# An adaLN block with linear attention: TensorE's order in phase 1 written out, state products in pairs, and x of the MLP's second pair loaded half a step sooner

## The chip, the cores and the metric

The kernel runs on one core of one Trainium2 chip. The metric is device time in microseconds; smaller is better. Before the change the median of three runs is 778.76 us (778.49 to 779.13). The engines are TensorE (PE, with its weight loads listed as PEld), VectorE (DVE), ScalarE (ACT), GpSimd (POOL) and SyncE (SP), which only issues DMAs here. Each engine works off its own list of instructions in order, and waits on semaphores for the others.

## The reference

The block gets 2048 tokens of width 640 and a conditioning vector c. All is float32.

```python
mod = (silu(c) @ w_mod).reshape(1, 6, 1, 640)
sa, ca, ga, sb, cb, gb = (mod[:, i] for i in range(6))
h = layernorm(x) * (1 + ca) + sa
x = x + ga * A(h)                  # attention
h = layernorm(x) * (1 + cb) + sb
x = x + gb * B(h)                  # MLP

def A(x):                          # 32 heads of 20
    q, k, v = heads(x @ wqkv)
    pq, pk = q @ w_phi, k @ w_phi
    phi_q = concat(softmax(pq), softmax(-pq))
    phi_k = concat(softmax(pk), softmax(-pk))
    kv = einsum("bhsf,bhsd->bhfd", phi_k, v)
    z = sum over tokens of phi_k
    o = (phi_q @ kv) / (phi_q . z + 1e-6)
    return o @ wo

def B(x):                          # F = 1728
    r = relu(x @ w1 + b1)
    return (r * r) @ w2 + b2
```

## The kernel before

The tokens stand in 16 tiles of 128 (`NT`), and two tiles make a pair `j`. Float32 products are made of three float32r products (`three`): both operands are split into a high part and a low remainder, and high x high, high x low and low x high are summed. So a projection of one token tile to 640 columns is 30 matmuls: two column parts of 384 and 256 (`CUT`), five chunks of the width, three products.

*Phase 1* folds `w_phi` into the weights of Q and K and then goes through the token tiles t. For each it makes K (`proj("k", t)`, copied by `to_sb`), V (`do_v`) and, for the first twelve, Q (`do_q`); the last four Q are postponed (`POSTPONED`). `spread` subtracts each head's maximum and minimum on VectorE, `exps` takes the exponentials on ScalarE, `k_norm` sums a key's 64 softmaxes and divides, `q_sums` sums a query's and takes the reciprocal into `rs_q`; the query's exponentials go to DRAM (`ESP`) undivided and are loaded again in phase 2 (`load_e`). `do_kv(t)` adds tile t's keys times values to the state, which stays in three PSUM banks (`kvp`, line 448): 11 products with 64 columns of weights, each two records in the profile. `t1(j, ...)` transposes the normalised x of a pair (tile `ta`), scales it on ScalarE and splits it into `hT`, the operand of the projections; all transposes go through one PSUM bank, `tp`. `ln_parts` is the layer norm of a pair.

Beside that, phase 1 makes four of the six modulation vectors (2, 3, 4 and 5; `mod_acc`, `mac`): five loads of 128 rows of `w_mod` each, accumulated on VectorE into one row tile with tag `s1`, of which there are five buffers, and then either summed over the partitions by a product with ones (`mod_rows`, tile `mr`, for the gates 2 and 5) or transposed and summed (`to_cols`, tile `mc`, for 3 and 4, the shift and scale of the second layer norm). It also scales `wo` with the gate and splits it (`prep_wo`). All this is one generator, `sides`, of which each token tile takes three steps (`SIDES`).

In the loop over t = 2 to 13 the order on every engine is the planner's: it goes by the order of the program, the buffers, and its own reckoning of when an operand is ready. `tc.issue_after(i)` keeps an instruction behind instruction i on its engine. From tile 14 on the order on TensorE, VectorE, ScalarE and GpSimd is written out by hand (`manual_schedule`), as it is ahead of the loop.

*Phase 2* takes the queries. `make_z` spreads the sums of the keys over the partitions (`zb`), `e_prod(t)` multiplies a query's exponentials by them and sums over each head (`dn`), GpSimd makes the denominator from it (`dd`), `e_recip` inverts it, `e_scale` scales the exponentials into `ezb`, and `tr_e` transposes them on TensorE (tile `te`) for the products with the state (`num`) and with `wo` (`do_wo`). The result of a tile goes to DRAM (`A1`).

*The MLP* takes the pairs j = 0 to 7. A pair has 14 half steps, each with one product up (`up`, 15 matmuls, then relu and square) and a part of one product down. For pairs 0 and 1 these are plain (`down_plain`). During pair j the next pair is made ready by `layer`: load the attention's result (`load_xm`) and x (`load_xx`), add them and store the sum (`add_x`, line 1019), normalise in six ScalarE passes (`ln_pieces`: two sums, two squares, two scalings), and transpose (`t2`, tile `tb`). A table gives the half step of each: `LN_AT0` is the one for the preparation of pair 1 during pair 0. `PREPS` says how many weight chunks are split and loaded in each half step of pair 0 (`prep`: split high, split low, load). SP's order is written out in pair 0 too.

Of the kernel before, what the change touches and what calls it, by code (L numbers as in the profile page):

```python
# [11 lines left out]
AF = mybir.ActivationFunctionType  # L12
# [3 lines left out]
P = 128  # L16
# [19 lines left out]
SIDES = 3  # L36
# [15 lines left out]
def kernel(  # L52
# [245 lines left out]
    def to_cols(acc, dest, nm):  # L298
        for c0, n in ((0, 4), (4, 1)):
            p = tp(f"mc{nm}_{c0}")  # L300
            for i in range(n):
                nc.tensor.transpose(p[:, i * P : (i + 1) * P], acc[:, (c0 + i) * P : (c0 + i + 1) * P], ident)
            nc.vector.tensor_reduce(
                dest[:, c0 : c0 + n], p[:, : n * P].rearrange("p (a b) -> p a b", b=P), axis=AX.X, op=ALU.add
            )
# [6 lines left out]
    def mod_acc(part):  # L312
        acc = None
        for k in range(NC):
            t = stage(part * D, k)
            mac(t, t, k, acc)
            acc = t
            yield None
        yield acc

    def mod_cols(part, dest):
        for acc in mod_acc(part):
            if acc is None:
                yield
        to_cols(acc, dest, part)
        yield

    def mod_rows(part, dest):
        for acc in mod_acc(part):
            if acc is None:  # L330
                yield
        for h in range(2):
            p = tp(f"mr{part}_{h}")
            nc.tensor.matmul(p[:, :HALF], ones, acc[:, h * HALF : (h + 1) * HALF], start=True, stop=True)
            nc.scalar.activation(dest[:, h * HALF : (h + 1) * HALF], p[:, :HALF], AF.Copy)
        yield
# [51 lines left out]
    def t1(j, *ds):  # L388
        if 0 in ds:
            HT[j] = ht(f"hT{j}", j)  # L390
        p = tp(f"ta{j}_{ds[0]}")
        for k, d in enumerate(ds):
            t_in(XB[j], d, p[:, 256 * k : 256 * k + 256])
        for k, d in enumerate(ds):
            t_out(cols_a, HT[j], d, f"a{j}", p[:, 256 * k : 256 * k + 256])

# [17 lines left out]
    def do_v(t):  # L414
        p = proj("v", t)
# [57 lines left out]
    def q_sums(t):  # L473
# [3 lines left out]
        nc.vector.reciprocal(s, s)  # L477
# [5 lines left out]
    def prep_wo(g, ga_b):  # L483
# [13 lines left out]
        nc.vector.tensor_tensor(t[:m], t[:m], ga_b[:m], op=ALU.mult)  # L497
# [5 lines left out]
    def side():  # L503
        ga_b = row("s4", "ga_b")
        yield from mod_rows(2, ga_b)
        for g in range(NG):
            prep_wo(g, ga_b)
            yield
        yield from mod_cols(3, cols_b[:, 0:5])
        yield from mod_cols(4, cols_b[:, 5:10])  # L510
        nc.vector.tensor_scalar(cols_b[:, 5:10], cols_b[:, 5:10], 1.0, None, op0=ALU.add)
        yield from mod_rows(5, gb_b)
        t = row("s1", "b2s")
        nc.sync.dma_start(t, bass.AP(tensor=b2.tensor, offset=b2.offset, ap=[[0, P], [1, D]]))
        nc.vector.tensor_tensor(bb, t, gb_b, op=ALU.mult)
        nc.sync.dma_start(b1_t, b1)
        yield

    sides = side()


# [154 lines left out]
    for e in (ET_.PE, ET_.DVE, ET_.Activation, ET_.Pool, ET_.SP):  # L676
        behind.enter_context(tc.issue_after(last[e]))
    q_chain(0)
    do_kv(0)
    k_norm(EK[1], 1)  # L680
    q_chain(1)
    for t in range(2, NT - 2):
# [4 lines left out]
        to_sb(proj("k", t), PK[t])  # L687
        norm = j + 1 if i == 0 and t < NT - 4 else j + 2 if t == NT - 5 else None
# [4 lines left out]
        do_v(t)  # L693
        if norm:
            next(parts)
        if t >= NT - 4:
            for ds in (((0, 1), (2, 3)) if i == 0 else ((4,),)):
                t1(j + 1, *ds)
# [16 lines left out]
        for _ in range(SIDES):  # L715
            next(sides, None)
    for _ in sides:
        pass
# [23 lines left out]
    exps(EQ[q0])  # L742
    q_sums(q0)
# [76 lines left out]
    def e_prod(t):  # L820
# [7 lines left out]
        nc.gpsimd.tensor_tensor(dn, dn, rs, op=ALU.mult)  # L828
        dd = DD[t] = small([P, H], "dd", f"dd{t}")
        nc.gpsimd.tensor_tensor(dd, dn[:, 0], dn[:, 1], op=ALU.add)  # L830
        nc.gpsimd.tensor_scalar(dd, dd, 1e-6, None, op0=ALU.add)

    def e_recip(t):
# [4 lines left out]
        nc.vector.tensor_tensor(DN[t], rs, DD[t][:, None, :].to_broadcast([P, 2, H]), op=ALU.mult)  # L838
# [568 lines left out]
    LN_AT0 = {"load": 3, "xx": 4, "add": (6, 7), "ln": (6, 7, 8, 8, 9, 9), 10: (0, 1), 11: (2, 3), 12: (4,)}  # L1407
# [3 lines left out]
    PREPS = iter([1, 3] + [2, 1] * 2 + [2, 2] + [1, 1] + [1, 2])  # L1411
# [198 lines left out]
```

## Time and profile before

| | us |
|---|---|
| median of three runs | 778.76 |
| lowest and highest | 778.49, 779.13 |
| profiled execution | 778.49 |
| its span, first to last instruction | 776.8 |
| TensorE busy | 768.9 |
| VectorE busy | 585.0 |
| ScalarE busy | 440.3 |
| GpSimd busy | 123.9 |

By stretches, phase 1's loop and its end stand between about 52 and 257 us, phase 2 from there to about 398 us, the MLP behind it. The page's rows give busy times; the timeline merges neighbouring instructions of one kind into a row with its start, its length and the count, and names in brackets the idle time ahead of it and what ended it. Matmuls are pipelined: the length of a row of matmuls reaches past the start of the next one, so the distance between two starts is what a row costs.

### The profile page before, as it was taken

How to read it: one execution, taken by the hardware profiler on the slowest of the kernel's cores; microseconds unless marked ns; L12 is line 12 of the kernel's file. 1: busy time of each engine (PE TensorE's matmuls, PEld its weight loads, DVE VectorE, ACT ScalarE, POOL GpSimd, SP SyncE). 2: the span in 40 equal slices, each digit the busy share in tenths (PEclk: the TensorE clock that was granted, in tenths of full speed). 3: DMA queues.
4: the chain of work that ended last, by engine and by line, in shares of the span. 5: the costliest groups of instructions: out<-in, count | busy, mean ns of one | idle time of the engine just before them, and what ended most of it. 6: DMA issues, size and time to landing. Idle time of an engine off the chain costs nothing.

```text
span 776.8 us, 15295 instructions
## 1 busy us (share of the span) xinstructions
PE 768.9 (99%) x5989; PEld 745.3 (96%) x5989; DVE 585.0 (75%) x1059; ACT 440.3 (57%) x991; POOL 123.9 (16%) x253
## 2 busy tenths in 40 slices
PE   9999999999999999999999999999999999999997
PEld 9999999999999988998999999999999999999997
DVE  6699899998788799986266667776767567585656
ACT  5766685486663355665875737446454645536331
POOL 3001101001100233221000001122221313213110
PEclk9999999999999999999999999999999999999999
DMA  9713245323120254222247456997666858667450
GB/s 331 294 68 132 84 143 169 133 99 108 69 101 3 88 168 170 85 85 103 85 135 256 137 174 226 290 318 251 187 195 205 236 178 261 188 191 209 128 172 35
DMA packets 50551, 126.03 MB, mean 162 GB/s; under 512 B 5991, under 2 KB 6759, under 8 KB 50479
## 3 DMA queue, kind: packets, MB, share of 16 engines
q1 hardware_dynamic: 33144, 83.99, 31.2%
q0 software_dynamic: 14752, 35.76, 16.5%
q10 hardware_dynamic: 2583, 5.30, 1.8%
q8 instruction: 47, 0.77, 0.4%
q14 instruction: 25, 0.20, 0.1%
HBM read 95.05 MB, written 29.88 MB: 161 GB/s over the span
## 4 chain that ended last, share of the span: by engine, by line
PE 96%; ACT 2%; DVE 1%; DMA 0%; issue 0%; SPq 0%; POOL 0%; ACTq 0%; POOLq 0%
PE up L78 23%; PE acc L78 17%; PE pwo L78 10%; PE pq L78 9%; PE pk L78 9%; PE pv L78 9%; PE acc3x L78 5%; PE kvp L448 3%; PE te L865 2%; PE tb L364 1%; PE numa L78 1%; PE foldk L280 1%; PE numc L78 1%; PE numb L78 1%; PE ta L364 1%; PE foldq L280 1%
## 5 line engine op out<-in xcount | busy, mean ns | idle before, releaser
L78 PE MATMUL up<-h,w 128*128 128x256 f32 x1640 | 206.5, 278 | 0.2 <-ACT ft L1184 0.2
L78 PEld LDWEIGHTS up<-h,w 128*128 128x128 f32 x1640 | 196.1, 188 | 0.3 <-ACT ft L1184 0.3
L1184 ACT ACTIVATE ft<-up,b_t 128x256 f32<-128x256 f32 x104 | 49.1, 472 | 116.0 <-PE up L78 115.5
L78 PE MATMUL acc<-w,ra 128*128 128x384 f32 x452 | 98.2, 336 | 0.0
L1185 DVE TENSOR_TENSOR ft<-ft 128x256 f32<-128x256 f32 x104 | 44.1, 424 | 54.2 <-ACT ft L1184 52.5
L78 PE MATMUL pwo<-wo,ot 128*128 128x256 f32 (+3 forms) x512 | 81.1, 312 | 0.0
L78 PE MATMUL pk<-wk,hT 128*128 128x384 f32 (+1 forms) x480 | 77.8, 312 | 0.2 <-ACT hT L376 0.2
L78 PEld LDWEIGHTS pwo<-wo,ot 128*128 128x128 f32 (+1 forms) x512 | 75.0, 188 | 2.7 <-issue 2.7
L78 PE MATMUL pv<-wv,hT 128*128 128x384 f32 (+1 forms) x480 | 75.9, 309 | 0.0
L78 PE MATMUL pq<-wq,hT 128*128 128x384 f32 (+1 forms) x480 | 74.9, 311 | 0.4 <-ACT k L424 0.4
L78 PEld LDWEIGHTS pk<-wk,hT 128*128 128x128 f32 x480 | 71.9, 188 | 1.9 <-ACT hT L376 0.8
L78 PEld LDWEIGHTS acc<-w,ra 128*128 128x128 f32 x452 | 72.6, 188 | 1.0 <-DVE ra L88 0.8
L78 PEld LDWEIGHTS pq<-wq,hT 128*128 128x128 f32 x480 | 70.8, 188 | 1.6 <-ACT k L424 0.9
L78 PEld LDWEIGHTS pv<-wv,hT 128*128 128x128 f32 x480 | 70.7, 188 | 0.4
L88 DVE TENSOR_TENSOR ra<-ft,ra 128x384 fp32r<-128x384 f32 (+2 forms) x86 | 36.8, 449 | 32.8 <-ACT ra L1208 20.2
L78 PE MATMUL acc3x<-w,ra 128*128 128x256 f32 x248 | 42.4, 278 | 0.0
L1208 ACT ACTIVATE ra<-ft 128x384 fp32r<-128x384 f32 x48 | 25.2, 526 | 28.4 <-DVE ft L1185 22.4
L78 PEld LDWEIGHTS acc3x<-w,ra 128*128 128x128 f32 x248 | 39.8, 188 | 0.2 <-DVE ra L88 0.2
L1294 POOL DMA_DIRECT2D ring_a<-td_a x34 | 18.2, 536 | 124.3 <-PE acc L78 102.7
L1199 DVE TENSOR_TENSOR ft<-ft 128x128 f32<-128x128 f32 x136 | 33.4, 287 | 1.2
L476 DVE TENSOR_REDUCE rs_q<-eq 128x64 f32<-128x1280 f32 x16 | 23.5, 1476 | 11.1 <-ACT eq L435 11.1
L828 POOL TENSOR_TENSOR dn<-dn,rs_q 128x64 f32<-128x64 f32 x16 | 8.7, 543 | 131.1 <-DVE dn L826 131.1
(256 smaller groups left out, 1414.2 us busy)
## 6 DMA issues: line engine op xcount, KB each, us to landing
ring_c<-td_c POOLq DMA_DIRECT2D x34, 384.0 KB, 4.1
ring_a<-td_a POOLq DMA_DIRECT2D x34, 384.0 KB, 4.0
ring_b<-td_b POOLq DMA_DIRECT2D x34, 256.0 KB, 3.8
esp<-eq SPq DMA_DIRECT2D x12, 640.0 KB, 2.9
el<-esp SPq DMA_DIRECT2D x12, 640.0 KB, 4.0
rw<-in_w SPq DMA_DIRECT2D x23, 320.0 KB, 3.3
wm<-in_w_mod SPq DMA_DIRECT2D x20, 320.0 KB, 3.9
xb<-in_x SPq DMA_DIRECT2D x8, 640.0 KB, 4.0
```

The costliest lines, as they stand in the source:

```text
L78: nc.tensor.matmul(o, a, b, start=first and i == 0, stop=last and i == len(terms) - 1, skip_group_check=skip,)
L88: (eng or nc.vector).tensor_tensor(out_lo, full, hi.bitcast(F32), op=ALU.subtract)
L280: nc.tensor.matmul(p[g // 3][:, (g % 3) * 120 : (g % 3) * 120 + n], r, bd_t[:120, g * 120 : g * 120 + n], start=True, stop=True,)
L364: nc.tensor.transpose(p[:, i * P : (i + 1) * P], xn[:, i, d * P : (d + 1) * P], ident)
L448: nc.tensor.matmul(kvp[g // 4][64 * c : 64 * c + 64, a : a + 2 * n].rearrange("p (s n) -> p s n", s=2), v[:, u], e[:, :, o : o + n], start ...
L476: nc.vector.tensor_reduce(s, heads(flat(e)), axis=AX.X, op=ALU.add)
L865: nc.tensor.transpose(p[:m, a : a + P], EU[2 * j + i][:, b : b + m], ident)
L1184: nc.scalar.activation(r, p, AF.Relu, bias=b1_t[:, f : f + 1])
L1185: nc.vector.tensor_tensor(r, r, r, op=ALU.mult)
L1199: nc.vector.tensor_tensor(t[:, o], t[:, a], t[:, b], op=op)
L1208: nc.scalar.activation(a[:, 0, :3], t[:, :3], AF.Copy)
L1294: nc.gpsimd.dma_start(RING[j, n, r], TD[n][r].bitcast(F32R))
```

## The change

1. **TensorE's order in the loop of phase 1 is written out** (`manual_schedule` for TensorE alone). For each tile: K, V, Q, with the transposes at stated places. The other engines' order stays with the planner.
2. **State products in pairs.** For even t, `do_kv(t - 2)` and `do_kv(t - 1)` follow the matmuls of V(t), and V's copies stand behind them. Tiles 12 and 13 are paired after K(15). Keys 14 and 15 use the query buffers `q0`, `q1`.
3. **Modulation at stated tiles.** The generator is gone. A table `SIDE` says which loads and accumulations a tile makes, now in the order 3, 4, gate 2, `wo`, gate 5. The accumulations and the products with the gate stay behind the newest VectorE instruction. The transposes of 3 and 4 follow the state products of t = 6 and 10 (four columns) and the transposes in Q(7) and Q(11) (the fifth); ScalarE copies them to a row tile, and one sum on VectorE replaces two. The gate's row products follow the state products of t = 8 and K(9); those of gate 5 stand behind K(15) and Q(12).
4. **No reciprocal of q's sums.** `rs_q` holds the sums. With sums r0, r1 and products n0, n1 the denominator becomes r0 r1 1e-6 + n0 r1 + n1 r0, six GpSimd operations instead of three, and each half is scaled by the other half's sum, two VectorE operations of 32 instead of one of 64.
5. **MLP.** During pair 0, x of pair 1 is loaded in half steps 2 and 3 instead of 3 and 4, added in 5 and 6 instead of 6 and 7, and normalised from 5 to 9 instead of 6 to 9; one weight preparation moves from half step 6 to 5.

```diff
+    def mod_turn(part, p, *cs_):
+        t = MT.setdefault(part, None) or row("s1", f"mt{part}")
+        MT[part] = t
+        a, n = cs_[0] * P, len(cs_) * P
+        for i, c in enumerate(cs_):
+            nc.tensor.transpose(p[:, i * P : (i + 1) * P], MA[part][:, c * P : (c + 1) * P], ident)
+        nc.scalar.activation(t[:, a : a + n], p[:, :n], AF.Copy)
+    def mod_sum(part, dest):
+        with tc.issue_after(newest(ET_.DVE)):
+            nc.vector.tensor_reduce(dest, MT[part].rearrange("p (a b) -> p a b", b=P), axis=AX.X, op=ALU.add)
+    def mod_mac(part, *ks):
+        for k, t in [(k, stage(part * D, k)) for k in ks]:
+            with tc.issue_after(newest(ET_.DVE)):
+                mac(t, t, k, MA.get(part))
+            MA[part] = t
+    def mod_row(part, dest, h):
+        p = tp(f"mr{part}_{h}")
+        c = slice(h * HALF, (h + 1) * HALF)
+        nc.tensor.matmul(p[:, :HALF], ones, MA[part][:, c], start=True, stop=True)
+        nc.scalar.activation(dest[:, c], p[:, :HALF], AF.Copy)
...
     def q_sums(t):
...
-        nc.vector.reciprocal(s, s)
...
+    AFTER_KV = {
+        6: lambda: mod_turn(3, tp("mc3"), 0, 1, 2, 3),
+        8: lambda: mod_row(2, ga_b, 0),
+        10: lambda: mod_turn(4, tp("mc4"), 0, 1, 2, 3),
+        12: lambda: t1(NT // 2 - 1, 2, 3),
+    }
+    LAST_COL = {7: (3, cols_b[:, 0:5]), 11: (4, cols_b[:, 5:10])}
+    SIDE = {
+        2: lambda: mod_mac(3, 0, 1, 2),
+        3: lambda: (mod_mac(3, 3, 4), mod_mac(4, 0)),
+        4: lambda: mod_mac(4, 1, 2),
+        5: lambda: (mod_mac(4, 3, 4), mod_mac(2, 0)),
+        6: lambda: mod_mac(2, 1, 2, 3),
+        7: lambda: mod_mac(2, 4),
+        8: lambda: None,
+        9: lambda: wo_weights(0, 1),
...
+        13: lambda: (mod_mac(5, 3, 4), biases()),
+    }
...
-    do_kv(0)
-    k_norm(EK[1], 1)
     q_chain(1)
+    pe = tc.manual_schedule(engines={ET_.PE})
+    pe.__enter__()
     for t in range(2, NT - 2):
...
         to_sb(proj("k", t), PK[t])
+        if t == NT - 4:
+            t1(j + 1, 0, 1)
+        if t == 9:
+            mod_row(2, ga_b, 1)
...
-        do_v(t)
+        p = proj("v", t, (1, 0, lambda: t1(j + 1, 4)) if t == NT - 3 else None)
+        if i == 0:
+            do_kv(t - 2)
+            do_kv(t - 1)
+            if t in AFTER_KV:
+                AFTER_KV[t]()
+        v_out(t, p)
...
         if i and t < NT - 4:
             t1(j + 1, 2, 3)
-            t1(j + 1, 4)
...
-        do_kv(t - 1)
         if t < NT - POSTPONED:
-            do_q(t)
+            do_q(t, (1, 3, lambda: t1(j + 1, 4, more=LAST_COL.get(t))) if i else None)
             q_chain(t)
         if i == 0 and t < NT - 4:
             t1(j + 1, 0, 1)
-        for _ in range(SIDES):
-            next(sides, None)
+        SIDE[t]()
+    pe.__exit__(None, None, None)
...
-        EK[t] = tok2("k", f"ek{t}")
+        EK[t] = tok2(f"q{t % 2}", f"ek{t}")
         spread(PK[t], EK[t], f"k{t}")
+    do_kv(ka - 2)
     do_kv(ka - 1)
+    mod_row(5, gb_b, 0)
     exps(EK[ka])
     k_norm(EK[ka], ka)
     do_q(q0)
+    mod_row(5, gb_b, 1)
...
     exps(EQ[q0])
+    nc.vector.tensor_tensor(bb, b2s[0], gb_b, op=ALU.mult)
     q_sums(q0)
...
-        nc.gpsimd.tensor_tensor(dn, dn, rs, op=ALU.mult)
         dd = DD[t] = small([P, H], "dd", f"dd{t}")
-        nc.gpsimd.tensor_tensor(dd, dn[:, 0], dn[:, 1], op=ALU.add)
-        nc.gpsimd.tensor_scalar(dd, dd, 1e-6, None, op0=ALU.add)
+        nc.gpsimd.tensor_tensor(dd, rs[:, 0], rs[:, 1], op=ALU.mult)
+        nc.gpsimd.tensor_scalar(dd, dd, 1e-6, None, op0=ALU.mult)
+        for s in range(2):
+            nc.gpsimd.tensor_tensor(dn[:, s], dn[:, s], rs[:, 1 - s], op=ALU.mult)
+            nc.gpsimd.tensor_tensor(dd, dd, dn[:, s], op=ALU.add)
...
         nc.vector.reciprocal(DD[t], DD[t])
-        nc.vector.tensor_tensor(DN[t], rs, DD[t][:, None, :].to_broadcast([P, 2, H]), op=ALU.mult)
+        for s in range(2):
+            nc.vector.tensor_tensor(DN[t][:, s], rs[:, 1 - s], DD[t], op=ALU.mult)
...
-    LN_AT0 = {"load": 3, "xx": 4, "add": (6, 7), "ln": (6, 7, 8, 8, 9, 9), 10: (0, 1), 11: (2, 3), 12: (4,)}
+    LN_AT0 = {"load": 2, "xx": 3, "add": (5, 6), "ln": (5, 6, 7, 7, 8, 9), 10: (0, 1), 11: (2, 3), 12: (4,)}
...
-    PREPS = iter([1, 3] + [2, 1] * 2 + [2, 2] + [1, 1] + [1, 2])
+    PREPS = iter([1, 3] + [2, 1, 2, 2, 1, 2] + [1, 1] + [1, 2])
```

More of the change, by code (lines that the diff above doesn't have):

```diff
@@ L296, in mac @@
             nc.vector.scalar_tensor_tensor(acc, t, cs[:, k : k + 1], prev, op0=ALU.mult, op1=ALU.add)
[L298 to L305, printed above, removed]
+    MT = {}
+    def mod_turn(part, p, *cs_):
[8 more added lines that the diff above has]
+            nc.vector.tensor_reduce(dest, MT[part].rearrange("p (a b) -> p a b", b=P), axis=AX.X, op=ALU.add)
     def stage(col, k):
@@ L310, in stage @@
         return t
[L312 to L336, printed above, removed]
+    MA = {}
+    def mod_mac(part, *ks):
[8 more added lines that the diff above has]
+        nc.scalar.activation(dest[:, c], p[:, :HALF], AF.Copy)
     def ln_parts(xt, nm, spare=None):
@@ L393, in t1 @@
             t_in(XB[j], d, p[:, 256 * k : 256 * k + 256])
+        if more:
+            mod_turn(more[0], p[:, 256:], 4)
         for k, d in enumerate(ds):
             t_out(cols_a, HT[j], d, f"a{j}", p[:, 256 * k : 256 * k + 256])
+        if more:
+            mod_sum(*more)
     def proj(nm, t, between=None):
@@ L414, in do_v, with v_out @@
     def do_v(t):
[L415 removed]
+        v_out(t, proj("v", t))
+    def v_out(t, p):
         v = vt[t % 2]
@@ L496, in prep_wo @@
         WO[g] = w
-        nc.vector.tensor_tensor(t[:m], t[:m], ga_b[:m], op=ALU.mult)
+        with tc.issue_after(newest(ET_.DVE)):
+            nc.vector.tensor_tensor(t[:m], t[:m], ga_b[:m], op=ALU.mult)
         nc.scalar.activation(w[:m, 0], t[:m], AF.Copy)
```

35 lines of the change are left out of this document (13 added, 22 removed).

## The prediction

> **What bounds the kernel now.** I read the page first, then the sums over stretches, then TensorE's timeline through phase 1, then the waits, and last the timelines of the other engines around TensorE's few gaps.
>
> ```profile
> span 776.8 us, 15295 instructions
> PE 768.9 (99%) x5989; PEld 745.3 (96%) x5989; DVE 585.0 (75%) x1059; ACT 440.3 (57%) x991; POOL 123.9 (16%) x253
> ...
> 52.30:144.10 91.80, 91.62 (x705) 89.60 (x705) 87.22 (x118) 60.33 (x139) 11.39 (x18) 1.00 0.38 127
> 68.30:82.60 14.30, 14.30 (x103) 14.29 (x102) 12.27 (x17) 9.84 (x23) 0.25 (x1) 1.00 0.20 74
> 52.30:257.10 204.80, 204.21 (x1601) 198.28 (x1600) 184.41 (x242) 125.53 (x294) 17.82 (x30) 1.00 0.30 102
> ```
>
> The last three rows are stretches (bounds and length, then busy time of PE, PEld, DVE, ACT, POOL, clock, DMA). TensorE is busy 99% of the span, and 204.21 of the 204.80 us from the first state products to the end of phase 1 (52.30 to 257.10), at full clock. VectorE is next with 184.41 us, 90%; before 144 it has 87.22 of 91.80, 95%. So the time is TensorE's own list of work, and what can be won is in the starts: a busy matmul row hides pipeline gaps, so I go by the distance from start to start.
>
> ```profile
> 62.48 0.69 PE L78 MATMUL pq<-wq,hT 128*128 128x384 f32 x3
> 63.10 1.38 PE L448 MATMUL kvp<-ek,vt 128*64 128x120 f32 x22
> 64.40 4.05 PE L78 MATMUL pq<-wq,hT 128*128 128x384 f32 x27
> 68.29 0.27 PE L364 MATMUL ta<-ident,xb 128*128 128x128 f32 x1
> ...
> 104.49 4.47 PE L78 MATMUL pv<-wv,hT 128*128 128x384 f32 x30
> 108.79 0.60 PE L364 MATMUL ta<-ident,xb 128*128 128x128 f32 x4
> 109.15 4.16 PE L78 MATMUL pq<-wq,hT 128*128 128x384 f32 x26
> ...
> 254.64 2.54 PE L448 MATMUL kvp<-ek,vt 128*64 128x120 f32 x44
> 257.11 1.86 PE L78 MATMUL pq<-wq,hT 128*128 128x384 f32 x9
> ```
>
> A projection of 30 matmuls that nothing interrupts takes 4.30 us (104.49 to 108.79). The same 30 with one state group put in take 0.62 + 3.89 = 4.51 us beside the group's own 1.30 (63.10 to 64.40): going in and out of the 64-column products costs 0.21 us. A single group costs 1.30 + 0.21 = 1.51 us. The double group that already stands at the end of phase 1 takes 2.47 us (254.64 to 257.11), with the same way in and out 2.68.
>
> **The change, part by part.**
>
> *Double state groups.* Token tiles 0 to 13 come singly now, 14 and 15 together; afterwards all come in pairs, seven new ones. Each saves 2 x 1.51 - 2.68 = 0.34 us, together **-2.4 us**, on the engine that sets the end. Above zero it can't go: the matmuls are the same.
>
> *TensorE in stated order.* It removes the places where the planner broke the order up:
>
> ```profile
> 123.70 0.45 PE L78 MATMUL pv<-wv,hT 128*128 128x384 f32 x2
> 124.33 4.58 PE L78 MATMUL pq<-wq,hT 128*128 128x384 f32 x30 [0.18 <-ACT k L424]
> ...
> PE pq L78 <- ACT k L424: 0.4, 2, 0.2
> PE pk L78 <- ACT hT L376: 0.2, 1, 0.2
> ...
> 220.42 0.62 PE L448 MATMUL kvp<-ek,vt 128*64 128x120 f32 x6
> ...
> 222.52 1.92 PE L78 MATMUL pk<-wk,hT 128*128 128x256 f32 x14
> ```
>
> K and V matmuls are interleaved there, so Q stands waiting for the copy that empties K's banks. 0.63 us pass for two matmuls that need about 0.29 (4.30 / 30 each), so 0.34 are lost; by the waits it happens twice, and once of that size for hT: about **-1.05 us**. In the new order V (4.30 us) lies between K's end and Q, and the last transposes of the next tile are issued after three matmuls of Q's second half instead of near its end, so these three go. One state group was split by four transposes: 2.10 us (220.42 to 222.52), where the group has 1.30 and four transposes 0.36 (108.79 to 109.15); with a second way out, half of the 0.21 above, that leaves **-0.35 us**. All other transposes and row products are the same in number.
>
> What the new order adds is waits that it can no longer avoid. State products t-1 follow V(t): K(t-1) has then V, Q, K, V, over 17 us, for softmax and scaling; VectorE's 87.22 us up to 144 are 14.5 for each of six tiles with all their other work, so the key's part is covered. The even tile's subtraction into its key buffer now waits for state product t-2, some 5.6 us after K(t), and queued behind it on VectorE are hT's low parts, which K(t+1) reads; Q's 4.30 us and VectorE's slack cover it. The copies of V wait for the same group on ScalarE (at most 1.30 us); the next projection into those banks is one projection later. One transpose bank serves all: each use waits for ScalarE's copy of the last, never closer than a half projection. One wait is tight, the gate's row sum at t=8, and it is my main rival:
>
> ```profile
> 82.59 2.35 PE L78 MATMUL pk<-wk,hT 128*128 128x384 f32 x15
> ...
> 89.86 1.48 DVE L476 TENSOR_REDUCE rs_q<-eq 128x64 f32<-128x1280 f32 x1
> ...
> 144.10 2.50 PE L78 MATMUL pk<-wk,hT 128*128 128x384 f32 x16
> ...
> 143.98 0.87 DVE L296 SCALAR_TENSOR_TENSOR wm<-wm,cs,wm 128x640 f32<-128x640 f32 x1
> ...
> 161.68 1.47 DVE L476 TENSOR_REDUCE rs_q<-eq 128x64 f32<-128x1280 f32 x1
> ```
>
> The last accumulation into it (0.87 us) is put behind the sums of Q(7). TensorE arrives one K, one V and one double group after Q(7), 4.30 x 2 + 2.68 = 11.3 us. The sums end 8.75 us after Q in the second stretch above (Q(3) ends at 82.59, sums at 91.34), where VectorE is 86% busy, but 19.05 us after it where it is full (144.10 to 163.15). So the wait is 0 (8.75 + 0.87 is below 11.3) or up to 19.05 + 0.87 - 11.3 = 8.6 us. Up to that point the change takes six reciprocals (0.54 us) and the six wo preparations (0.82 + 0.81 us, estimated from the 0.82 us products of that size) off VectorE and adds five accumulations: -3.2 - 9.8 + 4.4 = -8.6 us of 87.22, which is 86% again. I take the 86% row and 0. For small waits elsewhere, of the size of the three above, I add **+0.7 us** (ends 0 and 2).
>
> *Modulation at stated tiles.* The macs, loads and column sums are as many; four ScalarE copies of one bank or a quarter of it are new, on an engine with 125.53 of 204.80 us. The three loads in a row of gate weights find one or two free buffers of five and queue on SP; they have 30 us. The MLP gate's two row products move behind the last keys, the bias product into an idle time of VectorE: 0. Keys 14 and 15 in the q buffers let the first two reloads go earlier, but VectorE goes from the copies of zb to the first product without a pause, so 0.
>
> *No reciprocal of q's sums.*
>
> ```profile
> L477 DVE RECIPROCAL rs_q<-rs_q 128x64 f32<-128x64 f32 x12 | 6.4, 538 | 0.0
> ...
> 264.67 1.50 POOL L828 TENSOR_TENSOR dn<-dn,rs_q 128x64 f32<-128x64 f32 x1 [58.56 <-DVE dn L826]
> ...
> 267.60 0.32 POOL L828 TENSOR_TENSOR dn<-dn,rs_q 128x64 f32<-128x64 f32 x1 [0.69 <-DVE dn L826]
> 268.00 0.25 POOL L830 TENSOR_TENSOR dd<-dn 128x32 f32<-128x32 f32 x1
> 268.34 1.33 POOL L831 TENSOR_SCALAR dd<-dd 128x32 f32<-128x32 f32 x1
> ...
> 269.70 0.35 DVE L837 RECIPROCAL dd<-dd 128x32 f32<-128x32 f32 x1
> ...
> 271.68 0.23 DVE L850 TENSOR_TENSOR ezb<-el,dn 128x80 f32<-128x80 f32 x1
> ...
> 271.98 1.47 PE L865 MATMUL te<-ident,ezb 128*120 128x128 f32 x12
> ```
>
> Sixteen of 0.54 us leave VectorE, where nothing waits: 0. But POOL's chain per tile goes from three to six operations, four of them behind VectorE's sum (0.25 us and 0.1 us to the next), and a two-row product on VectorE becomes two. At the start of phase 2 this is on the path: tile 1's scaled features end at 271.91, and TensorE transposes them from about 272.2. POOL's third operation of tile 1 was drawn out to 1.33 us by the product on VectorE that ran till 269.7. Of the four operations one is caught the same way and two more (0.7 us) come after it; with the second small product (0.15) the features end at about 272.8: **+0.6 us** for TensorE. The Trainium skill (GPSIMD Engine Reference, Specifications) says that POOL shares its SBUF interfaces with VectorE and contends with instructions that have two SBUF inputs; the same operation at 1.50 and at 0.32 us agrees. Without such contention the four would end by 269.4 and the sum would be lower by 0.5; I keep the row. Later tiles: one product hides the chain, and the second transposes have over 1 us to spare.
>
> *x one half step sooner.*
>
> ```profile
> 427.12 0.68 PE L78 MATMUL acc<-w,ra 128*128 128x384 f32 x3
> ...
> 430.61 1.03 PE L78 MATMUL acc<-w,ra 128*128 128x384 f32 x3
> ...
> 433.63 0.55 PE L364 MATMUL tb<-ident,xm 128*128 128x128 f32 x3 [0.65 <-ACT xm L1430]
> ...
> 419.55 10.09 SPq L946 DMA_DIRECT2D rw<-in_w  x5
> 429.69 0.58 SPq L1020 DMA_DIRECT2D x<-xm  x1
> ...
> 429.08 0.46 ACT L1184 ACTIVATE ft<-up,b_t 128x256 f32<-128x256 f32 x1
> ...
> 432.66 0.92 ACT L1430 ACTIVATE xm<-xm,nbb,sqb 128x640 f32<-128x640 f32 x1 [0.46 <-DMA x<-xm]
> ```
>
> The last normalising pass waits till x1 has been stored, and that store stands on SP behind five weight loads which wait for buffers (10.09 us). Half a step sooner the store is issued before the blocked loads; the transposes' wait goes, 0.65 idle and 0.16 of restart (as above, 0.34 lost for 0.18 idle). The loads of x go past two weight loads on SP, the second half lands just before its addition, and one weight preparation moves forward so the queue stays filled. What is late next is the relu at 429.08: ScalarE has the same six passes, and a normalising pass held by POOL's statistics now stands ahead of this relu, by my count till 429.3. So the products that already run 0.35 us long at 430.61 (1.03 for 0.68) run some 0.25 longer. Net **-0.55 us** (ends -1.2 and +0.3).
>
> *Sum.* -2.4 - 1.05 - 0.35 + 0.7 + 0.6 - 0.55 = -3.05 us. The profiled execution took 778.49 us, 1.7 beside its span; the median 778.76 is 0.27 more. 778.76 - 3.05 is about **775.7 us**.
>
> **Rivals.**
> 1. *Gate row late (slower).* TensorE, in order, stands at t=8 behind the accumulation that follows Q(7)'s sums. Price L + 0.87 - 11.3 us for a lag L. For: VectorE's 19.05 us lag before. Against: the lag follows its load, and 86% had 8.75. At 19.05 us: 775.7 + 8.6 = 784.3. It makes the kernel slower than no change from L = 13.5 us on, and by over 0.2% from about 15. The Trainium skill (TensorE: Matmul & The Clock Gate, The HAM clock gate) adds that an idle window of about 3.4 us halves the clock for the next; by it some 1.7 us more. No run here shows so long a gap in phase 1.
> 2. *Gain eaten.* The planner lays VectorE and ScalarE anew; a lag L of about 12 to 15 us, or ten small waits of 0.34 us instead of two, leave 777.2 to 780.3. For: VectorE is at 90% over phase 1 and can't be passed by.
> 3. *More than forecast.* No new wait in phase 1 (-0.7), POOL not caught (-0.5), both MLP waits gone (-0.65): 773.8.
> 4. *The switch isn't saved:* pairs cost as two singles. Then 778.1; against it stands the row of 2.47 us.
>
> **How the numbers follow.** Forecast (774.3 to 777.1) 0.55, rival 3 0.13, rival 2 0.15, rival 1 0.14, rival 4 0.03. A measurement here tells 0.2%, 1.6 us, from no change: faster is below 777.2, 0.55 + 0.13 = 0.68; same 0.15 + 0.03 = 0.18; slower 0.14. The range, 773.4 to 779.4, leaves out rival 1's upper part and the last of 2 and 3; the likeliest case's own is 774.3 to 777.1.
>
> **What the profile after would show.** State groups of x44 with 2.5 us start to start; no wait of Q for K's copy; VectorE below 90% to the end of phase 1; a wait of te for ezb of about 0.6 us; no tb wait for xm, but acc above 1.03 us near 427. A long idle time before the mr product at t=8 would prove me wrong, as would hT or ek named among TensorE's waits with more than 2 us.

## The result

Twelve executions of the changed kernel took 781.21 us in the median (779.22 to 781.79), twelve of the kernel before, beside them, 778.5 us (778.16 to 779.13). The ratio is 1.0029, with a 95% interval of 1.0021 to 1.0038: slower by 2.7 us, where I forecast 775.7 and a range of 773.4 to 779.4. The profiled execution took 779.39 us. Page and sums over two stretches of the changed kernel (columns as in the prediction):

```profile
span 777.7 us, 15333 instructions
PE 765.6 (98%) x5989; PEld 744.1 (96%) x5989; DVE 580.2 (75%) x1057; ACT 443.6 (57%) x995; POOL 146.7 (19%) x301
...
51.70:197.76 146.06, 146.06 (x1150) 144.63 (x1148) 127.36 (x161) 97.33 (x223) 18.56 (x28) 1.00 0.28 97
197.76:258.13 60.37, 55.65 (x456) 53.23 (x454) 52.54 (x68) 31.54 (x76) 2.39 (x4) 1.00 0.39 130
```

TensorE had 0.6 us without work in phase 1 before. Now it has none for 146 us, and then 4.7 us in the last 60. Its timeline shows where (the second row is VectorE's):

```profile
152.88 0.81 PE L327 MATMUL mr<-wm,ones 128*128 128x320 f32 x2
...
151.81 0.88 DVE L295 SCALAR_TENSOR_TENSOR wm<-wm,cs,wm 128x640 f32<-128x640 f32 x1
...
198.12 3.26 PE L77 MATMUL pq<-wq,hT 128*128 128x384 f32 x18
202.01 0.44 PE L356 MATMUL ta<-ident,xb 128*128 128x128 f32 x2 [0.63 <-ACT hfa L367]
...
203.81 1.20 PE L77 MATMUL pk<-wk,hT 128*128 128x384 f32 x6
205.56 2.13 PE L77 MATMUL pk<-wk,hT 128*128 128x384 f32 x8 [0.55 <-ACT hT L368]
209.54 2.17 PE L77 MATMUL pk<-wk,hT 128*128 128x384 f32 x16 [1.85 <-DVE hT L87]
211.55 0.60 PE L356 MATMUL ta<-ident,xb 128*128 128x128 f32 x4
...
237.08 2.54 PE L446 MATMUL kvp<-ek,vt 128*64 128x120 f32 x44
241.22 0.81 PE L327 MATMUL mr<-wm,ones 128*128 128x320 f32 x2 [1.60 <-DVE wm L295]
```

K(12) takes 7.74 us from start to start (203.81 to 211.55) where a projection takes 4.30: 3.44 lost, waiting for hT of token pair 6. The row product of the MLP's gate comes 4.14 us after its state group instead of 2.47: 1.67 lost. In Q(11) the fifth transposes stand for the only transpose bank: Q(11) takes 5.69 us, against 4.81 in the last kernel below, where nothing stands: 0.88. Together 6.0 us, all behind 198 us. The row product at t=8, which I had feared, starts at 152.88 without a wait, but only 0.19 us after VectorE has ended the accumulation that it needs (151.81 + 0.88).

I cut every profiled execution at three of TensorE's products: the first Q product (33.40 us here), the first of Q(13), the first up product of the MLP. Lengths of the four parts in us:

| execution | time | to first Q | phase 1 from there | phase 2 | MLP |
|---|---|---|---|---|---|
| before | 778.49 | 33.89 | 223.22 | 140.54 | 379.13 |
| changed | 779.39 | 33.40 | 224.73 | 140.61 | 378.95 |
| changed, a second profile | 781.39 | 33.74 | 226.37 | 140.57 | 379.00 |

The first column of parts varies by itself (33.26 to 34.37 over all profiled executions of the document). So the profiled execution lost 1.5 us in phase 1: stops of 6.0, and so a gain of about 4.5 beside them. The columns behind phase 1 stay within 0.2. What the median lost beyond that is in the second profile.

### The profile page after: what moved, and what is told of

Read it like the earlier page. It is cut to its first block, busy times and chain, and to the rows that moved or that the text cites. A ratio compares the mean times of both kernels' runs of the same rounds, so it can differ in the third digit from the quotient of the medians.

```text
span 777.7 us, 15333 instructions
## 1 busy us (share of the span) xinstructions
PE 765.6 (98%) x5989; PEld 744.1 (96%) x5989; DVE 580.2 (75%) x1057; ACT 443.6 (57%) x995; POOL 146.7 (19%) x301
## 5 line engine op out<-in xcount | busy, mean ns | idle before, releaser
L77 PE MATMUL pk<-wk,hT 128*128 128x384 f32 (+1 forms) x480 | 73.7, 309 | 2.5 <-DVE hT L87 1.9
L77 PE MATMUL pv<-wv,hT 128*128 128x384 f32 (+1 forms) x480 | 72.3, 308 | 0.0
L437 DVE TENSOR_REDUCE sk<-ek 128x64 f32<-128x1280 f32 x16 | 23.7, 1482 | 16.0 <-ACT ek L432 13.4
L854 POOL TENSOR_TENSOR dn<-dn,rs_q 128x32 f32<-128x32 f32 x32 | 18.9, 592 | 74.0 <-DVE dn L848 73.8
```

Of the source, the lines that this page charges most:

```text
L77: nc.tensor.matmul(o, a, b, start=first and i == 0, stop=last and i == len(terms) - 1, skip_group_check=skip,)
L437: nc.vector.tensor_reduce(s, heads(flat(e)), axis=AX.X, op=ALU.add)
L854: nc.gpsimd.tensor_tensor(dn[:, s], dn[:, s], rs[:, 1 - s], op=ALU.mult)
```

## The experiments

**The changed kernel once more.**

> The changed kernel again, unchanged. Theory: TensorE's stops between 201 and 242 us cost 5.8 us in every execution (0.79 at the fifth transposes of pair 6, 3.3 in K(12) for hT, 1.67 for the gate's row product), which uses up the loop's gain of about 4.8 and leaves +0.6 to +0.9; and in most executions a stretch of about 3.4 us at half clock follows them, +1.7 us, so that the times stand in two groups, near 779.3 and near 781.3, and a profile of the second group has a dip of the granted clock in or after 201 to 242 us and nowhere else. Rival: the lower mean clock has nothing to do with those stops; then the dip lies elsewhere, or is spread over the span as a small loss everywhere.

Measured: 781.39 us (780.15 to 781.95, five executions), ratio 1.0036 (1.0024 to 1.0049). The stops lie at the same products, each as long within 0.02 us. Its sums over stretches:

```profile
207.64:211.05 3.41, 1.55 (x9) 1.24 (x10) 3.41 (x6) 0.49 (x1) 0.00 (x0) 1.00 0.09 37
211.05:214.46 3.41, 3.41 (x17) 3.41 (x16) 3.41 (x6) 1.52 (x4) 0.00 (x0) 0.50 0.31 96
241.77:245.18 3.41, 1.84 (x9) 1.68 (x10) 2.99 (x4) 1.00 (x3) 0.00 (x0) 1.00 0.79 240
```

The clock (third number from the right) is 0.50 for 3.41 us, and nowhere else in phase 1. The 3.41 us ahead of that had TensorE busy for only 1.55. Half of 3.41 us is 1.7; phase 1 is 1.64 longer than in the first profile. By their mean clock most executions pay this on top: of the 17 of the changed kernel, the three with a mean clock of 0.999 took 779.22 to 780.19, the others, at 0.996 to 0.998, 780.15 to 781.95.

**The MLP's edit alone.** In the kernel before:

```
-LN_AT0 = {"load": 3, "xx": 4, "add": (6, 7), "ln": (6, 7, 8, 8, 9, 9), ...
+LN_AT0 = {"load": 2, "xx": 3, "add": (5, 6), "ln": (5, 6, 7, 7, 8, 9), ...
-PREPS = iter([1, 3] + [2, 1] * 2 + [2, 2] + ...
+PREPS = iter([1, 3] + [2, 1, 2, 2, 1, 2] + ...
```

> The kernel before with only the MLP's edit: x of the first pair half a step sooner and the moved weight preparation. My prediction had -0.55 us for it. The traces of before and after give TensorE's excess over the run of the table as 1.20 us before (0.39 at acc, 0.81 at tb) and 1.18 after (all at acc, behind the scaling pass and the relu). Theory now: 0 to -0.2 us. Rival (the prediction's step): -0.5 us or more, if the acc wait is a product of the new phase 1 and not of the edit.

Measured: 778.01 us, ratio 0.9996 (0.9987 to 1.0005); the MLP part is 379.19 us long, against 379.13. No gain that shows. The changed kernel's timelines (TensorE, ScalarE) say why; the variant's have the same rows, 1.66 us sooner:

```profile
432.41 1.04 PE L77 MATMUL acc<-w,ra 128*128 128x384 f32 x3 [0.63 <-ACT ra L1233]
...
430.05 0.92 ACT L1455 ACTIVATE xm<-xm,nbb,sqb 128x640 f32<-128x640 f32 x1 [0.95 <-POOL nbb L1452]
```

The transposes' wait for xm is gone as forecast. But the scaling pass, held by POOL's statistics until 430.05, now stands ahead of the relu at 430.88, and acc waits 0.63 us for it, with a slow restart about what tb lost before. The prediction had this wait, at 0.25.

**The reciprocals alone.** In the kernel before:

```
-        nc.vector.reciprocal(s, s)
...
-        nc.gpsimd.tensor_tensor(dn, dn, rs, op=ALU.mult)
+        nc.gpsimd.tensor_tensor(dd, rs[:, 0], rs[:, 1], op=ALU.mult)
...
(POOL's longer chain and the split product as in the change)
```

> The kernel before with only the reciprocals of q's sums taken out and POOL's longer chain and the split product put in. Prediction's step: 16 reciprocals of 0.54 us leave VectorE where nothing waits, 0; the start of phase 2 loses 0.6 us: +0.6. Theory from the changed kernel's trace: there te stood 1.28 us instead of 1.23, so +0.05; VectorE's 6.4 us less load in phase 1 may take one of the three 0.34 us stops there: 0 to -0.4 in sum. Rival: the reciprocals are on the path in phase 1, then -1 us or more.

Measured: 778.39 us, ratio 1.0001 (0.9992 to 1.0009); phase 1 from the first Q 223.12 us, phase 2 140.57. Neither side of the trade is on the path.

**Less side work at tile 11.**

```
-        10: lambda: wo_weights(2, 3),
-        11: lambda: wo_weights(4, 5),
-        12: lambda: (... cols_b + 1 ..., mod_mac(5, 0, 1, 2)),
-        13: lambda: (mod_mac(5, 3, 4), biases()),
+        10: lambda: mod_mac(5, 0, 1, 2),
+        11: lambda: (mod_mac(5, 3, 4), biases()),
+        12: lambda: (... cols_b + 1 ..., wo_weights(2, 3)),
+        13: lambda: wo_weights(4, 5),
```

> The changed kernel with the side work of tiles 10 to 13 in another order: the gate's accumulations (5, 0 to 4) and the biases at t=10 and 11, four of the six wo preparations at t=12 and 13 instead of t=10 and 11. Theory: wo's products and copies are what puts hT of pair 6 behind on ScalarE and VectorE at t=11, and the last accumulation what the row product waits for. Then the 1.67 us at the row product go entirely, of the 4.1 us before t=12 most go, no dip of the clock stays, and the time is 773 to 775.5 us, with one group of times. Rival A: layer normalisation of pair 7, in the same stretch, is the cause: the stop in K(12) stays at over 2 us, and the time is 777 to 779.5. Rival B: the preparations only move their stop to K(13) or K(14): a new stop of over 1 us after 215 us, time 776 to 779.

Measured: 779.22 us, ratio 1.0010 (1.0001 to 1.0018). The row product no longer waits, but K(12) does, and the profiled execution had two stretches at half clock. TensorE's timeline and the sums over stretches:

```profile
207.79 0.61 PE L77 MATMUL pk<-wk,hT 128*128 128x384 f32 x2 [1.29 <-ACT hT L368]
210.06 3.25 PE L77 MATMUL pk<-wk,hT 128*128 128x384 f32 x13 [1.66 <-DVE hT L87]
...
205.14:208.55 3.41, 1.97 (x8) 0.97 (x7) 2.24 (x3) 2.60 (x8) 0.00 (x0) 1.00 0.79 273
208.55:211.96 3.41, 1.90 (x8) 1.90 (x9) 3.41 (x7) 0.55 (x2) 0.63 (x1) 0.50 0.00 0
211.96:215.38 3.42, 3.42 (x17) 3.42 (x16) 2.89 (x5) 2.34 (x5) 0.00 (x0) 0.50 0.63 234
```

So the four wo preparations moved away, with the gate's accumulations in their place, are not what delays hT: my theory (773 to 775.5 us) fell here, and rival A stood. What is left at tile 11 is the normalisation of token pair 7, which only this odd tile carries. ScalarE's timeline in the changed kernel, and VectorE's behind it:

```profile
198.35 0.83 ACT L341 ACTIVATE junka<-xb,sma 128x640 f32<-128x640 f32 x1
...
200.92 1.03 ACT L367 ACTIVATE hfa<-ta,cols_a 128x256 f32<-128x256 f32 x2
...
203.08 1.75 ACT L347 ACTIVATE xb<-xb,nba,sqa 128x640 f32<-128x640 f32 x2
...
205.07 0.74 ACT L368 ACTIVATE hT<-hfa 128x256 fp32r<-128x256 f32 x2
...
206.22 1.48 DVE L437 TENSOR_REDUCE sk<-ek 128x64 f32<-128x1280 f32 x1
207.62 0.81 DVE L426 TENSOR_REDUCE mxq<-q 128x32 f32<-128x640 f32 x1
...
209.07 0.42 DVE L87 TENSOR_TENSOR hT<-hfa,hT 128x256 fp32r<-128x256 f32 x1
```

The transposes for d=2, 3 are done at 198.1; their hT comes at 205.07, behind squares and scaling passes, and the last low part at 209.07, behind sums and maxima. K(12) begins at 203.81.

**Normalisation of pair 7 later.**

```
-        norm = j + 1 if i == 0 and t < NT - 4 else j + 2 if t == NT - 5 else None
+        norm = j + 1 if i == 0 and t < NT - 4 else None
...
             q_chain(t)
+        if t == NT - 5:
+            layer_norm(XB[j + 2], f"a{j + 2}")
...
(transposes of pair 7: d=0, 1 after the states of tile 12, d=2, 3 after K(13))
```

> The changed kernel with one thing moved: layer normalisation of token pair 7 is issued after Q(11) instead of inside tile 11, and pair 7's transposes come one projection later (d=0, 1 after the states of tile 12, d=2, 3 after K(13)). The side work of tiles 9 to 13 stays as it was. The previous run moved four wo preparations and the gate's accumulations, and K(12) still stood 3.7 us for hT. Theory now: at tile 11 ScalarE has the six normalising passes of pair 7 (4.9 us) ahead of hT of pair 6, and TensorE in stated order has only Q(11) between those transposes and K(12). So here the stops in K(12) and before it (4.1 us) shrink below 1 us, the row product's 1.67 us stays, the dip of the clock goes in most executions: 775 to 776.5 us. Rival: wo's products and copies are enough by themselves: the stop in K(12) stays over 2 us, 778 us or more. Second rival: the stop moves to pair 7's own hT, at K(14): over 1 us there, 776.5 to 778.

Measured: 778.61 us, ratio 0.9997 (0.9987 to 1.0007). TensorE's and VectorE's timelines, and stretches:

```profile
203.80 4.75 PE L77 MATMUL pk<-wk,hT 128*128 128x384 f32 x30
...
216.11 2.40 PE L446 MATMUL kvp<-ek,vt 128*64 128x120 f32 x22 [1.95 <-DVE ek L439]
...
211.83 0.54 DVE L438 RECIPROCAL sk<-sk 128x64 f32<-128x64 f32 x1
212.29 0.76 DVE L426 TENSOR_REDUCE mxk<-k 128x32 f32<-128x640 f32 x1
...
213.69 0.87 DVE L295 SCALAR_TENSOR_TENSOR wm<-wm,cs,wm 128x640 f32<-128x640 f32 x1
214.48 1.48 DVE L439 TENSOR_TENSOR ek<-ek,sk 128x1280 f32<-128x1280 f32 x1
...
212.79:216.20 3.41, 1.46 (x25) 1.33 (x26) 3.41 (x5) 0.94 (x4) 0.00 (x0) 1.00 0.60 212
216.20:219.61 3.41, 3.41 (x27) 3.24 (x28) 3.41 (x5) 0.01 (x1) 0.00 (x0) 0.50 0.22 81
240.09:243.51 3.42, 1.82 (x11) 1.58 (x10) 3.10 (x5) 0.90 (x2) 0.00 (x0) 1.00 0.87 301
```

K(12) now runs in 4.59 us (203.80 to 208.39), with the wo preparations still in tile 11: the normalisation was the cause of its stop. But the time went down by 2.6 us only, not to the 775 to 776.5 that I expected. The row product's 1.6 us stay, as expected, and a stop that the trace had hidden comes out: the state group of tile 11 waits 1.95 us for VectorE to scale ek(11). The scaling stands behind the maxima and minima of K(12) and an accumulation, though its reciprocal was ready at 212.4.

**Both moves together.** The last two diffs in one kernel.

> Both moves together: normalisation of pair 7 after Q(11), and the gate's accumulations at tiles 10 and 11 with four wo preparations at 12 and 13. Theory: nothing over 0.5 us is left of TensorE's stops in phase 1, the clock stays full, and the loop's gain shows whole: 773 to 774.5 us, 4 to 5.5 below the kernel before, in one group. Rival: K(14) now waits for hT of pair 7 behind the wo copies: 775 to 778.

Measured: 778.47 us, ratio 1.0000 (0.9991 to 1.0009): my 773 to 774.5 was wrong by 4 us. The same state group now stands 3.02 us, because a wo product, an accumulation and the sums of Q(11) lie on VectorE ahead of that scaling, and the profiled execution had half clock from 216.05 to 222.88. Moving work out of one queue's way put it in another's.

**TensorE's order left to the planner.** In the changed kernel:

```
-    pe = tc.manual_schedule(engines={ET_.PE})
-    pe.__enter__()
...
-    pe.__exit__(None, None, None)
```

> The changed kernel without the stated order of TensorE: the planner orders it, all else as it is. In the kernel before, hT of pair 6 is as late (its last low part ends at 211.15, 3.5 us after K(12) begins at 207.63), but the planner lets V(12) and K(12) alternate, so that nothing stands still. Theory: with the order free, K and V of tile 12 alternate again and the stop of 3.3 us there shrinks below 1 us; the stops of Q for K's copy come back (2 to 4 of 0.34 us). Time 776 to 778. Rival: the stops come from the load of ScalarE and VectorE whatever TensorE's order; then TensorE stops as long as before, 779 or more.

Measured: 781.31 us, ratio 1.0031 (1.0018 to 1.0044). The stop in K(12) is gone, as the theory said, for K and V alternate. This was so before the change, when hT came as late: the timelines of the kernel before from the start of K(12), TensorE's and behind them VectorE's:

```profile
207.63 1.77 PE L78 MATMUL pk<-wk,hT 128*128 128x384 f32 x11
...
209.59 0.71 PE L78 MATMUL pv<-wv,hT 128*128 128x384 f32 x3
...
208.94 0.42 DVE L88 TENSOR_TENSOR hT<-hfa,hT 128x256 fp32r<-128x256 f32 x1 [1.50 <-ACT hT L376]
...
210.74 0.41 DVE L88 TENSOR_TENSOR hT<-hfa,hT 128x256 fp32r<-128x256 f32 x1
```

But two other stops take its place in the planner-ordered variant, and a half-clock stretch follows the longer one:

```profile
229.02 6.45 PE L77 MATMUL pk<-wk,hT 128*128 128x384 f32 x46 [1.53 <-DVE hT L87]
...
241.04 0.97 PE L327 MATMUL mr<-wm,ones 128*128 128x320 f32 x2 [3.08 <-DVE wm L295]
...
238.16:241.57 3.41, 0.53 (x3) 0.46 (x3) 3.41 (x5) 0.00 (x0) 0.00 (x0) 1.00 0.95 351
241.57:244.98 3.41, 3.41 (x12) 3.22 (x11) 2.10 (x3) 1.69 (x3) 0.00 (x0) 0.50 0.58 225
```

So the stated order turns late hT into a stop, but the queues' load is the deeper cause: the theory's 776 to 778 was too low, and the rival nearer.

**The attention's gate first.** The parts of the modulation in the order 2, 3, 4, 5:

```
+        2: lambda: mod_mac(2, 0, 1, 2),
+        3: lambda: (mod_mac(2, 3, 4), mod_mac(3, 0)),
+        4: lambda: mod_mac(3, 1, 2),
+        5: lambda: wo_weights(0, 1),
+        6: lambda: (wo_weights(2), mod_mac(3, 3, 4)),
+        7: lambda: wo_weights(3, 4),
+        8: lambda: (wo_weights(5), mod_mac(4, 0, 1, 2)),
+        9: lambda: mod_mac(4, 3, 4),
+        10: lambda: mod_mac(5, 0, 1, 2),
+        11: lambda: (mod_mac(5, 3, 4), biases()),
+        12: lambda: ... cols_b + 1 ...,
+        13: lambda: None,
...
(the row products and transposes that use these parts move with them)
```

> The changed kernel with the modulation's parts in another order: the gate of the attention first (tiles 2 to 5), the six wo preparations at tiles 5 to 8, the columns after, the MLP's gate accumulated at tiles 10 and 11; normalisation of pair 7 stays inside tile 11. No wo preparation is left after tile 8. Theory (normalisation of pair 7 is the cause): the row product's 1.67 us goes, K(12) still stands 2 us or more, the clock still dips: 776.5 to 779.5. Rival (wo preparations are the cause): no stop over 0.5 us at tile 12: 773 to 774.5. Third: the wo preparations make new stops between tiles 5 and 9, where VectorE was 95% busy before: some of 0.3 to 1 us there.

Measured: 780.88 us, ratio 1.0030 (1.0020 to 1.0040). With no wo preparation after tile 8, K(12) still loses 2.3 us (207.01 to 213.59, less 4.30), as the theory said. But there are two new stops, at tile 10 and so later than the third case had them, and the time is above the 776.5 to 779.5 that I expected. One is 0.88 us for hT in K(10), the other:

```profile
187.83 0.63 PE L304 MATMUL mc<-ident,wm 128*128 128x128 f32 x4 [2.52 <-DVE wm L295]
```

**The gate's rows later.**

```
     do_kv(ka - 1)
-    mod_row(5, gb_b, 0)
...
     do_q(q0)
-    mod_row(5, gb_b, 1)
+    mod_row(5, gb_b, 0)
...
     do_v(ka)
+    mod_row(5, gb_b, 1)
```

> The changed kernel with only the two row products of the MLP's gate moved: one from before Q(12) to after it, the other from after Q(12) to after V(14). Theory: the 1.67 us at the row product go, the 4.1 us around K(12) stay, and so does the dip of the clock in most executions, since it follows the stops in K(12): two groups, near 777.7 and 779.5, median 779.2 to 780. Rival: the dip needs the second stop; then one group near 777.7.

Measured: 779.21 us (777.85 to 780.04), ratio 1.0009 (1.0000 to 1.0018): 2.0 us less than the changed kernel, by the stop of 1.67. K(12)'s stop and the half-clock stretch behind it (0.50 from 211.65 to 215.06) stay.

**All of it cleared.**

```
(pair 7 later and the gate's rows later, as above)
+        8: lambda: mod_mac(5, 0, 1, 2),
+        9: lambda: (mod_mac(5, 3, 4), wo_weights(0)),
+        10: lambda: wo_weights(1, 2),
+        11: lambda: None,
+        12: lambda: ... cols_b + 1 ...,
+        13: lambda: (wo_weights(3, 4, 5), biases()),
...
             k_norm(EK[t], t)
+        scaled = newest(ET_.DVE)
...
-            q_chain(t)
+            with tc.issue_after(scaled) if t == NT - 5 else ExitStack():
+                q_chain(t)
```

> The changed kernel with all causes named so far taken out of the queues around tile 11: normalisation of pair 7 after Q(11) and its transposes one projection later; no side work at tiles 11 and 12 (the MLP's gate accumulated at tiles 8 and 9, wo preparations at 9, 10 and 13); VectorE scales the key of tile 11 before it touches Q(11), since in the last runs the state products after V(12) stood 2.0 and 3.0 us for that scaling behind Q's work and wo's; the gate's row products after Q(12) and V(14). Theory: the queues of ScalarE and VectorE around tile 11 are all there is; no stop over 0.5 us is left in phase 1, phase 1 ends 4.5 to 5 us sooner than in the changed kernel, the clock stays full, 773 to 774.5 us in one group. Rival: the load itself is too much for the stated order, and the stop moves on once more, to tile 12, 13 or 14: 776 or more.

Measured: 774.04 us (773.48 to 774.36), ratio 0.9944 (0.9931 to 0.9956): 4.5 us faster than the kernel before and 7.2 faster than the changed one. TensorE's timeline:

```profile
199.05 3.26 PE L77 MATMUL pq<-wq,hT 128*128 128x384 f32 x18
...
203.86 4.46 PE L77 MATMUL pk<-wk,hT 128*128 128x384 f32 x30
208.16 4.46 PE L77 MATMUL pv<-wv,hT 128*128 128x384 f32 x30
212.55 2.54 PE L446 MATMUL kvp<-ek,vt 128*64 128x120 f32 x44
```

K(12) takes 4.30 us, V(12) 4.39, and the state group follows at once. Phase 1 from the first Q takes 219.27 us, 3.95 less than before; no stop is left in it, its clock is 1.00 throughout, and the five times lie within 0.9 us. This is the loop that I had priced.

**Its pairs and its order taken back.** Two variants of this kernel. One takes state groups singly, the other leaves TensorE's order to the planner, by the edit shown above:

```
-        if i == 0:
-            do_kv(t - 2)
-            do_kv(t - 1)
+        if t == 2:
+            do_kv(0)
+        do_kv(t - 1)
...
-    do_kv(ka - 2)
     do_kv(ka - 1)
```

> The last kernel, in which TensorE no longer stops, with the state groups of tiles 2 to 13 taken singly again, each behind V of the next tile, instead of six pairs. Prediction's step: a pair saves 2 x 1.51 - 2.68 = 0.34 us, so six are worth 2.0 us and this one takes 776.0 us. Rival (the prediction's fourth): the way in and out of the 64-column products isn't saved by pairing; then it takes 774.0 as before. By the trace: 22 products of a single group and the way in and out take 1.51 us from start to start.

> The same kernel without TensorE's stated order; the planner orders it with the same queues of work. Prediction's step: the planner's breaking up of projections costs 1.05 us (three of 0.34), and the split state group 0.35; so 775.2 to 775.5, with Q's waits for K's copies back. Rival: with VectorE and ScalarE relieved the planner's alternation of K and V is free of loss, 774.0. Second rival: it meets a new late hT, as the changed kernel did without the stated order (1.87 us in K(13)): 776 or more.

Measured: 776.71 us with single groups, ratio 0.9976 (0.9967 to 0.9985), phase 1 from the first Q 221.91: 2.64 us more than with the six pairs, 0.44 for each. Not all of this is the pairs'. TensorE's timeline with pairs, two rows, and behind them with single groups:

```profile
82.42 4.46 PE L77 MATMUL pk<-wk,hT 128*128 128x384 f32 x30
...
112.22 4.46 PE L77 MATMUL pk<-wk,hT 128*128 128x384 f32 x30
...
83.07 4.46 PE L77 MATMUL pk<-wk,hT 128*128 128x384 f32 x30
...
113.21 4.46 PE L77 MATMUL pk<-wk,hT 128*128 128x384 f32 x30
...
152.61 1.38 PE L446 MATMUL kvp<-ek,vt 128*64 128x120 f32 x22
...
154.92 0.81 PE L327 MATMUL mr<-wm,ones 128*128 128x320 f32 x2 [0.94 <-DVE wm L295]
```

From K(4) to K(6) nothing differs but the groups: 29.80 us with a pair, 30.14 without, so a pair saves 0.34. At t=8 the gate's row product, rival 1 of the prediction, now does wait: TensorE arrives sooner, and the product starts 2.31 us after its group instead of 1.30. Six times 0.34 and this 1.01 would make 3.05; the rest is scatter between two profiles, which differ by 0.24 us even from the first Q to K(2) (18.56 with pairs, 18.32 without), where the work is the same.

With the planner's order 774.98 us, ratio 0.9950 (0.9936 to 0.9963), phase 1 220.47: the stated order is worth 1.20 us there, 0.9 in the medians. Q's waits for K's copies, which I expected back, did not come back: from the first Q to the end of phase 1 this variant's list of TensorE's waits names only 0.22 us for hT, in K(14). K(14) and K(15) take 9.33 us there instead of 8.86, and K(12), V(12) and a state group that is split again 11.53 instead of 11.16.

## Why the prediction was wrong

- **Double groups, -2.4:** right. 0.34 us each from K(4) to K(6), as priced; the 0.44 by the whole of phase 1 holds a wait for the gate's row besides. The Trainium skill (TensorEngine Tiling (Array Packing), Key Properties) says that a change of tiling mode drains TensorE; that the pair saves a way in and out agrees, and the section gives no figure.
- **TensorE in stated order and the split group, -1.4:** right in size (1.20 us by the phase), and by its mechanism only in part. The waits of Q for K's copy are gone in the changed kernel, but in the cleared kernel the planner's order doesn't bring them back: there 0.37 us are lost about a split state group, which was priced at 0.35, and 0.47 in K(14) and K(15). That the sizes meet is partly luck. (Three of 0.34 are 1.02, where the prediction has 1.05.)
- **Small waits of the new order, +0.7 (ends 0 and 2):** this is the step that failed. The stops came to 6.0 us, of which 4.3 belong here (K(12) 3.44, Q(11) 0.88) and 1.67 to the next term. Of hT's low parts the prediction said that Q's 4.30 us and VectorE's slack cover them, and of the one transpose bank that at least half a projection lies between two uses. At tile 11 the slack was not there, and half a projection was not enough: ScalarE's copy of the transposes at 197.76 began at 200.92. I went through the waits for keys, banks and V copies with the load of early tiles, where indeed there is none up to 198 us, and through the gate row at t=8. I did not go through tile 11, where three things meet: normalisation of pair 7 on ScalarE, a VectorE full of sums, maxima and side work, and K(12), which in the stated order follows Q(11) at once. Of these the normalisation is shown to be the cause in K(12). The row that could have told it stood in the trace of before: the last low part of hT of pair 6 ended at 211.15 there, 3.5 us after K(12) had begun, and only the alternation with V(12), a kind of order that I had counted as a loss to be removed, hid it. The last transposes themselves came late there, at 209.25; but the low part ahead of it, from transposes at 201.39, also ended at 209.36 only, 1.7 us after K(12)'s start.
- **Modulation at stated tiles, 0:** wrong by 1.67 us. The last accumulation for the MLP's gate stands on VectorE (240.30 to 241.17) behind the scaling of a key and the first passes over keys 14 and 15, and the row product is asked for right after the state group. I named this mechanism for the gate at t=8 (rival 1) and gave the same pattern at the other gate nothing. At t=8 the 0 came true by 0.19 us, which is luck: the lag of Q(7)'s sums was 10.17 us (141.72 to 151.89), not the 8.75 that I took, and with single groups the product stood there for 0.94 us.
- **Clock:** I had it inside rival 1 only. It took 1.64 us in the second profile, and by their mean clock most executions have it.
- **Reciprocals, +0.6:** mis-sized. te stood 1.28 us from start to start instead of 1.23, and phase 2 as a whole lost 0.03 in the variant with this edit alone. The held POOL operation is there, but only one operation comes behind it instead of two, and the others of the chain follow every 0.2 to 0.4 us; the scaled features of tile 1 end 0.4 us later (15.18 us after the start of Q(13) against 14.80), not 0.9, and TensorE loses 0.05. The held one in the changed kernel's timeline of POOL:

```profile
269.21 1.45 POOL L854 TENSOR_TENSOR dn<-dn,rs_q 128x32 f32<-128x32 f32 x1
```

- **x half a step sooner, -0.55:** mis-sized; 0 within 0.2. The wait moved from tb to acc almost whole, and not by a quarter of it.
- **Sum.** With every stop cleared phase 1 gains 3.95 us, against 3.8 in the prediction (2.4 + 1.05 + 0.35). So close a match is partly luck, for profiles scatter by more: 0.5 us of the difference between this and the 4.5 of the changed kernel lies ahead of K(4), where the two do the same work (48.62 us from the first Q against 48.11). The gain was real and was spent: in the changed kernel 4.5 of gain less 6.0 of stops makes +1.5 us, and with the half-clock stretch that most executions have +3.1; 2.7 were measured. Of the signs that I named for being wrong, hT among TensorE's waits came, at tile 12, at 1.85 us in one wait and 3.44 in all. Rival 1 had the right mechanism, a stated order that makes TensorE stand behind a full queue, at the wrong place.

## What to carry to other kernels

An order that is written out for the bounding engine takes away the freedom that hid late inputs, so for each product of the new order ask when its last input comes in the trace of before, and count alternation there as cover, not only as loss. Side work at stated tiles must be checked at the fullest tile of every queue it enters, not at the average; in this kernel one odd tile with an extra normalisation decided. Moving one crowding item shows the next, so clear the queue's order (what stands ahead of the needed instruction) and not only its load.

## What the runs showed of the hardware

The granted clock went to 0.50 for 3.41 us, once or twice in a row, after a stretch of 3.41 us in which TensorE was busy for only 1.55, 1.97, 1.46 or 0.53 us; after 1.82 and 1.84 us it stayed at 1.00. TensorE need not stand still the whole stretch: one stop of 1.95 us was enough. The same stops were followed by half clock in the second profile of the changed kernel and not in the first. The Trainium skill (TensorE: Matmul & The Clock Gate, The HAM clock gate) describes windows of about 3.4 us that run free of the kernel's start and a halving after an idle one. The length and the halving agree, and the difference between two executions with equal stops fits windows that fall differently; that the window must be idle does not, and where the border lies is open, since 1.97 was followed by half clock and 1.82 was not. By the next column, the busy time of the weight loads, the same stretches do fall apart: 0.46 to 1.33 us ahead of half clock, 1.58 and 1.68 where the clock stayed. Six rows are too few for a rule.
